# Warming products on any free PSUM bank until the seventh f-tile, and attention pairs of the third batch on in a fixed order

## The chip, the cores and the metric

One core of one Trainium2 chip runs the whole problem. The engines named here are TensorE (PE, whose weight loads the profile lists apart as PEld), VectorE (DVE), ScalarE (ACT), GpSimd (POOL) and SyncE (SP), which issues nearly all transfers. The metric is device microseconds of one execution, shown as a median of a few runs; one further execution was profiled, and all rows below come from that one.

## The reference

The program is an attention with fixed masks, followed by a gated two-layer network on its result. All inputs and the output are float32 (the two weight matrices arrive as float64 numbers, because they were divided by a NumPy square root).

```python
def _attn_ref(q, k, v):                       # q, k, v: (8 batches, 8 heads, 576, 64)
    scores = scale * np.matmul(q, k.transpose(0, 1, 3, 2))
    rel = pos[:, None] - pos[None, :]
    mask_local = (rel >= 0) & (rel < 32)                       # heads 0-3
    mask_strided = (rel >= 0) & (pos[None, :] % 32 == pos[:, None] % 32)   # heads 4-7
    scores = np.where(masks, scores, -1e9)
    attn = softmax(scores)
    return np.matmul(attn, v)

def _moe_ref(x, w_in, w_out):                 # x: (4608, 512), w_in: (512, 2048), w_out: (2048, 512)
    h = x @ w_in
    sp = np.maximum(h, 0.0) + np.log1p(np.exp(-np.abs(h)))
    return (h * erf(sp)) @ w_out
```

## The kernel before

**Attention** is done a pair of heads at a time: `heads(b, hp, ...)` for batch `b` (0 to 7) and head pair `hp` (0 and 1 local mask, 2 and 3 strided), 32 pairs in all, written here as 1.3 for batch 1, pair 3. Each pair has: two loads (queries and keys, values), `scores` on PE with the mask added by a product with the identity (the first 8 pairs) or by DVE (the rest), the row maximum (DVE, L408), the exponential (ACT, L429 or, piece by piece with its sum, L444), the reciprocal of the sum (L462, L463) and the scaling by it (POOL or DVE, L470), the transposes on PE (`turn`, L479), their copy to SBUF (ACT, L485), the product with the values (`av`, L498), and the split of the result into a high part (ACT, L517) and a low part (DVE, L522) that the network reads as `xhi` and `xlo`. There are four such pairs of tiles, one for each head pair, each with a ring of two batches.

**The network** works on 12 chunks of 384 tokens by 16 tiles of 128 hidden features: 192 f-tiles. `ftile` has 12 products of 384 columns (`mm1`, L641: high times high, high times low, low times high), eleven pointwise steps that alternate between ACT (L649, L679) and DVE (L646, L676, L682), the last of which writes `glo`, and nine products of 512 columns into the three output banks `o0`, `o1`, `o2` (`mm2`, L712). Three PSUM banks (`h`) hold the f-tiles under way, so the first product of f-tile 3 waits for `glo` of f-tile 0. The first three chunks are cut into segments of 4, 4 and 8 features, so that the first 12 f-tiles need only 4 + 4 of the 32 weight tiles. A weight tile is loaded as 64-bit words and becomes two float32 tiles: three bit operations on DVE (L591, L598, L604), a cast on ACT (L609) and a difference on DVE (L612). `wN` is tile N: 0 to 15 are `w_in`, 16 to 31 `w_out`.

**SBUF and PSUM at the start.** The first two batches are computed before any f-tile can run, and seven of their eight pairs borrow room: `home` names weight tiles whose SBUF place holds the pair's queries, keys, values and probabilities first, so the load of, for example, `w14` (home of pair 1.2) can only be issued once `av` of pair 1.2 is done. `banks` names the PSUM banks they use: those of `h`, `o0`, `o1`, `o2`, or the two banks `ps`.

**What sets the order.** Nothing is written out by hand. Every piece of work is an `Op` with an engine, a duration, a key, and the buffers and ops it depends on. `Plan.order` is a list scheduler: on each engine it looks at the first `WINDOW` ops by key, takes the one that can start soonest in its own model of time, and among those that can start within 2 ns the one with the lowest key. The result is the fixed order of instructions of each engine; on the chip each engine then works strictly down its list, and SP its list of transfers. The keys are tables of numbers: `KP` (one row a pair, with seven steps), `KW` (weight tiles), `FT` (steps of an f-tile), and `PRO + SLOT * k` for f-tile k.

**The filler.** When the planner finds PE idle it can put in a warming product: one bf16 product of the identity with 512 columns of constants (L824), whose result nobody reads. Before the change it writes one buffer in bank `o2`, and it ends with the first pair that uses that bank (pair 0.3):

```python
first = plan.add("pe", 0.217, -10.0, warm, o_con, [warm_ps])
plan.filler = (first, warm, warm_ps, o2_first[0])
```

There are 14 of them.

Of the kernel before, what the change touches and what calls it, by code (L numbers as in the profile page):

```python
# [38 lines left out]
)  # L39
KP = (  # L40
    (20.3287, 53.91, -160.53, 18.1965, -47.9251, -48.4351, -45.9709),
    (-11.5867, -179.324, 278.004, -56.864, 29.5817, 111.268, -24.2757),
    (-37.2881, -285.525, 218.382, -3.34506, -147.536, -61.349, -160.866),
    (-3.30041, -73.2783, 113.183, 4.45478, -53.4418, -218.264, -9.86919),
    (18.4971, -63.2216, 140.85, -145.013, -40.5878, -375.486, -97.5485),
    (26.9473, -194.862, 187.13, -211.888, 100.567, -144.206, -385.178),
    (29.3598, 112.224, 34.5004, -139.626, -186.803, -311.65, -205.587),
    (40.629, -47.3516, -107.951, -152.785, -94.4726, -260.703, -328.673),
    (145.421, -29.1371, 101.451, 215.325, 141.627, 232.353, 147.006),
    (156.959, 213.968, -86.1117, 167.748, 197.693, 69.8737, 215.036),  # L50
    (214.158, 122.935, 213.19, 328.996, 214.474, 18.278, 173.207),
    (192.057, 302.789, 389.825, 207.406, 286.075, 210.654, 231.419),
    (311.012, 303.593, 285.037, 162.499, 316.839, 302.425, 213.801),
    (300.253, 202.803, 308.604, 234.138, 294.599, 227.375, 455.083),
    (234.305, 484.755, 266.452, 59.4845, -388.072, 255.135, 34.835),
    (365.686, 279.095, 257.584, 136.31, 289.522, 279.315, 239.144),
    (311.964, 379.917, 360.165, 318.437, 277.972, 289.912, 313.896),
    (398.277, 419.169, 405.134, 540.378, 463.219, 414.175, 410.718),
    (374.266, 340.595, 412.97, 365.306, 312.772, 421.745, 367.034),
    (400.873, 504.293, 447.42, 525.942, 542.714, 477.305, 404.891),  # L60
    (429.56, 205.119, 452.221, 477.615, 588.077, 437.589, 433.417),
    (434.951, 395.537, 444.904, 412.829, 464.795, 438.451, 436.011),
    (454.859, 440.736, 485.38, 513.585, 478.737, 465.682, 432.45),
    (466.926, 593.721, 523.838, 503.643, 416.953, 481.072, 489.414),
    (570.321, 596.524, 584.59, 533.102, 568.713, 632.717, 665.278),
    (481.13, 245.48, 404.828, 533.548, 417.461, 534.902, 474.017),
    (532.709, 540.879, 495.504, 473.216, 767.743, 414.442, 503.973),
    (602.088, 614.688, 620.304, 610.44, 682.554, 676.756, 678.331),
    (605.431, 617.475, 664.962, 621.689, 662.639, 578.048, 547.039),
    (690.641, 695.65, 723.32, 466.891, 705.997, 650.07, 429.58),  # L70
    (645.282, 705.753, 703.317, 687.525, 662.029, 631.987, 690.823),
    (700.543, 703.075, 661.128, 671.32, 528.806, 628.088, 603.928),
)
# [850 lines left out]
```

## Time and profile before

| | us |
|---|---|
| median of 3 runs (lowest, highest) | 938.94 (937.38, 939.02) |
| the profiled execution's own time | 937.39 |
| its span, first to last instruction | 935.6 |
| PE busy | 908.6 |
| DVE busy | 683.3 |
| ACT busy | 660.2 |
| POOL busy | 61.2 |
| first product of f-tile 0, of f-tile 3 | 49.92, 69.73 |
| first `mm2` | 71.93 |

Times in the rows are microseconds from the start of the span. A row of the timeline gives start, duration, engine, line, operation, what it writes and reads, and how often it stands there in a run; durations of PE and DVE rows overlap the next row's start a little, so the step from start to start is what an instruction costs its engine. A row of windows gives, for a stretch, the busy time of each engine with its number of instructions, the granted clock of PE (1.00 is full, 0.50 half), the busy share of the 16 DMA engines, and GB/s moved. In the page's slices a digit is tenths of one fortieth of the span (23.4 us).

### The profile page before, as it was taken

To read this page: it belongs to the slowest core of one execution; us is meant where nothing else is said; L and a number is where in the kernel's file an instruction comes from. 1 tells how busy PE (TensorE), PEld (TensorE's weight loads), DVE (VectorE), ACT (ScalarE), POOL (GpSimd) and SP (SyncE) were. 2 spreads that over 40 slices of the span, in tenths; PEclk is the share of its full clock that TensorE was granted. 3 is DMA by queue.
4 is the path that set the end of the run, shared out by engine and by line. 5 is a ranking of instruction groups with operands and counts; after the bars stand their busy time and mean duration, and the time that the engine had idled before them with its cause. 6 is when DMAs were issued, how large, how long until landed. Compare 5 with 4: busy or idle time off the path is not lost.

```text
span 935.6 us, 20064 instructions
## 1 busy us (share of the span) xinstructions
PE 908.6 (97%) x8157; PEld 810.6 (87%) x8158; DVE 683.3 (73%) x1355; ACT 660.2 (71%) x1478; POOL 61.2 (7%) x58
## 2 busy tenths in 40 slices
PE   4789999999999999999999999999999999999998
PEld 3578899988888899998898888989898888999997
DVE  6779999997588667657677686676776776666664
ACT  5667888777667767667676766766766767766765
POOL 1200012111112000000010000000100000000000
PEclk9589999999999999999999999999999999999999
DMA  9967114312415011001204111000211110000000
GB/s 346 350 246 291 39 61 66 64 29 50 97 54 143 18 46 61 0 28 64 72 27 140 41 53 55 35 27 18 89 46 46 62 56 18 34 1 1 34 1 34
DMA packets 23421, 68.86 MB, mean 74 GB/s; under 512 B 2592, under 2 KB 3232, under 8 KB 23328
## 3 DMA queue, kind: packets, MB, share of 16 engines
q1 hardware_dynamic: 20736, 62.86, 18.9%
q0 software_dynamic: 2592, 4.72, 3.6%
q8 instruction: 64, 1.05, 0.5%
q14 instruction: 29, 0.24, 0.1%
HBM read 53.41 MB, written 14.16 MB: 72 GB/s over the span
## 4 chain that ended last, share of the span: by engine, by line
PE 90%; DVE 5%; DMA 2%; issue 1%; ACT 0%; POOL 0%; SPq 0%; POOLq 0%; DVEq 0%
PE h L641 41%; PE o L712 41%; PE s L372 3%; PE x L498 3%; PE t L479 2%; DVE a L646 1%; DMA v<-v_loc 1%; DMA qk<-qk_loc 1%; PE s L498 1%; DVE pair L612 1%; DVE w L598 0%; DMA qk<-qk_str 0%; PE s L479 0%; DVE w L604 0%; DVE b L646 0%
## 5 line engine op out<-in xcount | busy, mean ns | idle before, releaser
L712 PE MATMUL o<-pair,ghi 128*128 128x512 f32 x1152 | 360.3, 394 | 0.0
L641 PE MATMUL h<-xhi,pair 128*128 128x384 f32 x1536 | 303.4, 340 | 0.3 <-DVE glo L682 0.2
L641 PEld LDWEIGHTS h<-xhi,pair 128*128 128x128 f32 x1536 | 270.1, 189 | 12.1 <-DVE glo L682 2.4
L712 PEld LDWEIGHTS o<-pair,ghi 128*128 128x128 f32 x1152 | 211.1, 188 | 36.0 <-ACT ob L727 0.4
L649 ACT ACTIVATE b<-b 128x384 f32<-128x384 f32 x384 | 201.1, 525 | 44.8 <-DVE b L646 40.7
L712 PE MATMUL o<-pair,glo 128*128 128x512 f32 x576 | 224.6, 390 | 0.0
L641 PE MATMUL h<-xlo,pair 128*128 128x384 f32 x768 | 165.1, 337 | 0.0
L646 DVE SCALAR_TENSOR_TENSOR a<-a,h 128x384 f32<-128x384 f32 x192 | 105.8, 551 | 70.5 <-ACT b L649 70.2
L649 ACT ACTIVATE a<-a 128x384 f32<-128x384 f32 x192 | 101.1, 527 | 75.5 <-DVE a L646 74.9
L682 DVE TENSOR_TENSOR glo<-h,ghi 128x384 fp32r<-128x384 f32 x192 | 106.5, 555 | 54.0 <-ACT ghi L679 53.6
L649 ACT ACTIVATE a<-h 128x384 f32<-128x384 f32 x192 | 93.3, 486 | 72.4 <-PE h L641 71.4
L646 DVE SCALAR_TENSOR_TENSOR a<-h,a 128x384 f32<-128x384 f32 x192 | 106.6, 555 | 44.0 <-ACT a L649 43.6
L676 DVE TENSOR_TENSOR h<-b,h 128x384 f32<-128x384 f32 x192 | 107.2, 558 | 43.0 <-ACT b L649 42.7
L641 PEld LDWEIGHTS h<-xlo,pair 128*128 128x128 f32 x768 | 136.6, 189 | 0.0
L712 PEld LDWEIGHTS o<-pair,glo 128*128 128x128 f32 x576 | 108.1, 188 | 23.3
L679 ACT CAST ghi<-h 128x384 fp32r<-128x384 f32 x192 | 90.9, 473 | 34.8 <-PE o L712 27.6
L646 DVE SCALAR_TENSOR_TENSOR b<-b,a 128x384 f32<-128x384 f32 x192 | 106.7, 556 | 2.5
L649 ACT ACTIVATE b<-a 128x384 f32<-128x384 f32 x192 | 100.6, 524 | 2.9
L470 POOL TENSOR_TENSOR sm<-sm,r 128x768 f32<-128x768 f32 (+3 forms) x35 | 45.4, 1298 | 633.2 <-DVE r L463 512.3
L408 DVE TENSOR_REDUCE mx<-s 128x12 f32<-128x768 f32 (+3 forms) x37 | 28.9, 786 | 8.0 <-PE s L385 7.7
L727 ACT COPY ob<-o 128x512 f32<-128x512 f32 x54 | 31.2, 587 | 4.2 <-PE o L712 4.0
L372 PEld LDWEIGHTS s<-qk 64*32 64x32 f32 (+1 forms) x1616 | 21.2, 117 | 11.6 <-issue 5.0
(49 smaller groups left out, 513.9 us busy)
## 6 DMA issues: line engine op xcount, KB each, us to landing
out<-ob SPq DMA_DIRECT2D x36, 256.0 KB, 2.0
v<-v_loc SPq DMA_DIRECT2D x13, 640.0 KB, 3.8
words<-w_out SPq DMA_DIRECT2D x16, 512.0 KB, 8.8
words<-w_in SPq DMA_DIRECT2D x16, 512.0 KB, 7.9
qk<-qk_loc SPq DMA_DIRECT2D x13, 592.0 KB, 3.8
qk<-qk_str SPq DMA_DIRECT2D x12, 608.0 KB, 4.1
v<-v_str SPq DMA_DIRECT2D x16, 384.0 KB, 3.1
out<-ob POOLq DMA_DIRECT2D x18, 256.0 KB, 4.6
```

Source lines behind the costliest of these rows:

```text
L372: yield nc.tensor.matmul(bank(s, h)[m * j : m * (j + 1), 64 * t : 64 * (t + 1)], queries(rows, q0, m), keys_of(rows, q0), start=(h, j) not ...
L408: yield nc.vector.tensor_reduce(out=mx[:, parts[i], :units], in_=wide(of(s, i)), axis=mybir.AxisListType.X, op=ALU.max)
L470: yield (nc.gpsimd if pool_norm else nc.vector).tensor_tensor(out=d, in0=d, in1=spread(rc, i), op=ALU.mult)
L498: yield nc.tensor.matmul(bank(px, m)[h * D : (h + 1) * D, a * n : (a + 1) * n], values(rows, (2 * a + h) * D), pt[rows, h, c : c + n], sta ...
L641: yield nc.tensor.matmul(ph[:, :CH], win[4 * s + cc][:, w, fs], x[cc][:, c0 : c0 + CH], start=(i == 0), stop=(i == len(terms) - 1))
L646: yield nc.vector.scalar_tensor_tensor(out=out, in0=in0, scalar=scalar, in1=in1, op0=op0, op1=op1)
L649: yield nc.scalar.activation(dst, src, func, bias=bias[i], scale=scale)
L676: yield nc.vector.tensor_tensor(out=ph[:, :CH], in0=bb.tile, in1=ph[:, :CH], op=ALU.mult)
L679: yield nc.scalar.copy(ghi.tile, ph[:, :CH])
L682: yield nc.vector.tensor_tensor(out=glo.tile, in0=ph[:, :CH], in1=ghi.tile.bitcast(F32), op=ALU.subtract)
L712: yield nc.tensor.matmul(po.tile, g[:, ts], wout[f][:, w], start=(f == first_f and i == 0), stop=(f == last_f and i == 2),)
L727: yield nc.scalar.copy(ob.tile, po.tile)
```

## The change

Three things change in the code. A warming product is no longer tied to one buffer: `_spare` asks, for each of the tags `o2`, `o1`, `o0` and `ps`, whether the last buffer there has no user left at that time, and the filler makes a new buffer on the first such bank. The filler ends with `mm1` of the seventh f-tile (`mm1_first[6]`) and no longer with pair 0.3. And the pairs from batch 2 on (those that are not `own`) are chained: each pair's loads, scores, transposes and value products come after the same step of the pair before (`turns`). The planner's look-ahead `WINDOW` goes from 250 to 400, and all its tables (`PRO`, `SLOT`, `FT`, `KW`, `KP`) are replaced.

```diff
-PRO = 40
-SLOT = 4.3
+PRO = 41
+SLOT = 4.59
 BACKLOG = 1.1130116
-FT = (-10.5854, -2.40059, 6.35438, 31.1122, -70.6188, 13.8691, 84.3288, 11.3161, 2.23209, -15.3397, 0.274502, 44.5287)
+FT = (0.289363, -24.4893, -7.52371, 20.6488, -54.5891, -7.75633, 107.462, 111.082, -9.24549, -68.1746, -106.267, 36.4614)
...
-    (700.543, 703.075, 661.128, 671.32, 528.806, 628.088, 603.928),
+    (-30, -22.5012, -29.7906, -30, -30, -28.8058, -28.8058),
...
-    WINDOW = 250
+    WINDOW = 400
...
+    def _spare(self, tag, live, now):
+        order = live.get(tag)
+        return not order or all(
+            u.end is not None and u.end + (self.SAME if u.eng == "pe" else self.LATENCY)["pe"] <= now
+            for u in order[-1].users
+        )
...
                 if e == "pe" and self.filler and self.filler[0].end is not None:
-                    can.append((max(free[e], self.filler[0].end + 0.2), 1e9, e, -1))
+                    soon = max(free[e], self.filler[0].end + 0.2)
+                    spare = [tag for tag in self.filler[2] if self._spare(tag, live, soon)]
+                    if spare:
+                        can.append((soon, 1e9, e, -1))
...
-                o = Op(e, 0.217, 0.0, self.filler[1], (), (), (self.filler[2],), 0.0)
+                x, emit = self.filler[1](next(tag for tag in self.filler[2] if self._spare(tag, live, t)))
+                o = Op(e, 0.217, 0.0, emit, (), (x,), (), 0.0)
...
+        if not own:
+            for name, o in (("q", lq), ("v", lv), ("s", o_s), ("t", o_t), ("x", o_v)):
+                if name in turns:
+                    o.after.append(turns[name])
+                turns[name] = o
...
-    warm_ps = buf("ps_o", f"o{NTT - 1}", [P, DM], "warm")
-
-    def warm():
-        yield nc.tensor.matmul(warm_ps.tile, ident_b, con[:, :512], start=True, stop=True)
-
-
-    first = plan.add("pe", 0.217, -10.0, warm, o_con, [warm_ps])
-    plan.filler = (first, warm, warm_ps, o2_first[0])
+    def warm(tag):
+        n = len(plan.ops)
+        w = buf("ps_a", "ps", [P, 2, 512], f"warm{n}") if tag == "ps" else buf("ps_o", tag, [P, 512], f"warm{n}")
+
+        def run():
+            yield nc.tensor.matmul(w[:, 0, :] if tag == "ps" else w[:, :], ident_b, con[:, :512], start=True, stop=True)
+
+        return w, run
+
+    w, run = warm("o2")
+    first = plan.add("pe", 0.217, -10.0, run, o_con, [w])
+    plan.filler = (first, warm, ("o2", "o1", "o0", "ps"), mm1_first[6])
```

The lists of instructions show what the planner makes of it. Lines that are 11 to 17 higher in the changed kernel are the same statements (L498 is L509 there, L641 is L658, L712 is L729, L824 is L841). The first place is PE where the opening passes into the f-tiles. Names carry the batch and pair (`s_1_3` are the scores of pair 1.3, `h_0` is f-tile 0); only the first row of a run that repeats is shown. Before:

```order
L641 MATMUL h_0_787<-xhi0_76,pair0_363 128x384
L372 MATMUL s_1_3_816<-qk30_1_3_622,qk29_1_3_621 64x64 x24
L498 MATMUL s0_1_0_575<-qk11_1_0_286,v_1_0_368 64x32 x2
L641 MATMUL h_1_899<-xhi0_76,pair0_363 128x384
L641 MATMUL h_2_971<-xhi0_76,pair0_363 128x384
L498 MATMUL s_1_3_816<-qk29_1_3_621,v_1_3_687 64x54 x22
L641 MATMUL h_3_1103<-xhi0_76,pair0_363 128x384
```

And with the change:

```order
L383 MATMUL s_1_3_851<-qk30_1_3_738,qk29_1_3_737 64x64 x24
L509 MATMUL s0_1_0_629<-qk11_1_0_545,v_1_0_675 64x32 x2
L841 MATMUL warm3794_927<-con_85 128x512
L841 MATMUL warm3803_1007<-con_85 128x512
L658 MATMUL h_0_1073<-xhi0_76,pair0_943 128x384
L658 MATMUL h_1_1113<-xhi0_76,pair0_943 128x384
L509 MATMUL s_1_3_851<-qk29_1_3_737,v_1_3_883 64x54 x22
L658 MATMUL h_2_1203<-xhi0_76,pair0_943 128x384
L841 MATMUL warm3824_1278<-con_85 128x512
L658 MATMUL h_3_1313<-xhi0_76,pair0_943 128x384
L658 MATMUL h_4_1339<-xhi0_76,pair0_943 128x384
L729 MATMUL o0_0_1364<-pair16_549,ghi_0_1283 128x512 x2
```

The scores of pairs 1.3 and 1.2 and the value products of pair 1.0 have moved ahead of f-tile 0, and f-tile 4 and the scores of pair 2.0 ahead of the first `mm2`. The rows of warming products stand for 9 (ahead of the scores of pair 1.2), 21 and 10 of them; there are 82 in the changed kernel.

The second place is DVE around the `glo` of the first two f-tiles. Before:

```order
L646 SCALAR_TENSOR_TENSOR a_1_988<-a_1_988,h_1_899 128x384
L682 TENSOR_TENSOR glo_0_1043<-h_0_787,ghi_0_1032 128x384
L646 SCALAR_TENSOR_TENSOR a_2_1005<-h_2_971,a_2_1005 128x384
L646 SCALAR_TENSOR_TENSOR b_1_1018<-b_1_1018,a_1_988 128x384
L612 TENSOR_TENSOR pair19_995<-w32_19_966,pair19_995 128x512
L598 SCALAR_TENSOR_TENSOR w32_6_968<-words6_730,w32_6_968 128x512
L522 TENSOR_TENSOR xlo3_83<-s_1_3_816,xhi3_79 128x18x18
L522 TENSOR_TENSOR xlo3_83<-s_1_3_816,xhi3_79 128x18x14
L676 TENSOR_TENSOR h_1_899<-b_1_1018,h_1_899 128x384
```

And with the change:

```order
L621 SCALAR_TENSOR_TENSOR w32_7_1135<-words7_776,w32_7_1135 128x512
L699 TENSOR_TENSOR glo_0_1298<-h_0_1073,ghi_0_1283 128x384
L693 TENSOR_TENSOR h_1_1113<-b_1_1220,h_1_1113 128x384
L615 SCALAR_TENSOR_TENSOR w32_23_1139<-words23_843,w32_23_1139 128x512
L663 SCALAR_TENSOR_TENSOR a_2_1272<-a_2_1272,h_2_1203 128x384
L699 TENSOR_TENSOR glo_1_1332<-h_1_1113,ghi_1_1329 128x384
L663 SCALAR_TENSOR_TENSOR b_2_1311<-b_2_1311,a_2_1272 128x384
L608 TENSOR_SCALAR w32_14_1337<-words14_1222 128x512
L629 TENSOR_TENSOR pair7_1304<-w32_7_1135,pair7_1304 128x512
```

More stands ahead of `glo_0` than before (the splits of pairs 1.3 and 1.2, one weight tile, two steps of f-tiles 1 and 2), less between `glo_0` and `glo_1`, and the first bit operation on weight tile 14 now follows two rows after `glo_1`; before, it comes some 70 rows later.

The third place is the list of transfers that SP issues, around tile 14. Before:

```order
L585 DMA words12_1075<-w_in 128x1024
L358 DMA v_2_0_1118<-v_loc 128x1280
L585 DMA words14_1130<-w_in 128x1024
L585 DMA words15_1146<-w_in 128x1024
L585 DMA words27_1169<-w_out 128x1024
```

And with the change:

```order
L602 DMA words10_1171<-w_in 128x1024
L602 DMA words30_1199<-w_out 128x1024
L602 DMA words14_1222<-w_in 128x1024
L602 DMA words15_1274<-w_in 128x1024
L361 DMA qk_2_1_1290<-qk_loc 128x1184
```

The load of tile 14 keeps its place among the last weight tiles (it needs the room of pair 1.2), and has moved ahead of tile 12 in the list.

More of the change, by code (lines that the diff above doesn't have):

```diff
@@ L26 @@
 SW = 512
-PRO = 40
-SLOT = 4.3
+PRO = 41
+SLOT = 4.59
 BACKLOG = 1.1130116
-FT = (-10.5854, -2.40059, 6.35438, 31.1122, -70.6188, 13.8691, 84.3288, 11.3161, 2.23209, -15.3397, 0.274502, 44.5287)
+FT = (0.289363, -24.4893, -7.52371, 20.6488, -54.5891, -7.75633, 107.462, 111.082, -9.24549, -68.1746, -106.267, 36.4614)
 KI = 6.0
 KW = (
[4 rows of a table removed]
[4 rows of a table added]
 )
 KP = (
[L41 to L71, printed above, removed]
-    (700.543, 703.075, 661.128, 671.32, 528.806, 628.088, 603.928),
@@ new lines @@
+    (8.72531, 15.3266, 49.3756, 8.39434, 9.71023, 16.0435, 40.2649),
+    (-33.2667, -32.4582, -25.2032, -4.71525, 23.3634, 38.5999, -34.6194),
+    (-3.32722, 14.171, 65.6986, 22.708, 5.7846, -0.90524, -6.13492),
+    (-0.845554, 25.7345, 14.5624, 4.32498, 9.67501, 24.2441, 58.6052),
+    (27.1808, 31.0972, 28.9995, -1.24966, -22.602, 24.5694, -9.17578),
+    (12.7444, 8.33475, 64.1615, 7.47789, 24.3066, 31.2506, -7.37547),
+    (59.1669, 75.8282, 35.2304, 54.1156, 3.55879, 6.30503, 1.44202),
@@ new lines @@
+    (48.539, 42.13, 43.9807, 7.065, 28.0374, 12.7742, 20.1927),
+    (62.9708, 118.313, 65.7316, 109.482, 135.689, 178.053, 214.067),
+    (123.636, 279.712, 105.738, 148.596, 187.83, 145.11, 237.33),
+    (133.667, 215.051, 137.96, 168.378, 198.152, 176.116, 238.661),
+    (142.144, 208.148, 235.957, 308.305, 263.348, 272.387, 283.229),
+    (247.917, 257.392, 254.975, 251.721, 255.925, 267.187, 270.083),
+    (245.277, 289.199, 303.979, 299.482, 291.447, 309.453, 340.687),
+    (287.063, 331.064, 291.825, 315.285, 298.122, 317.411, -28.8058),
@@ new lines @@
+    (300.054, -18.1776, 308.518, 308.574, 313.179, 338.852, -5.16791),
+    (302.28, 24.0747, 350.314, 380.417, 330.366, 13.1796, 0.905989),
+    (368.813, 1.91996, 389.598, 30, 26.6243, 11.6485, 30),
+    (388.986, 23.6787, 26.4176, 30, 30, 30, 30),
+    (-30, 22.7877, 22.7877, -9.32161, 7.48325, 22.7877, -4.17841),
+    (30, -29.3034, -29.3034, -30, 28.8694, 30, -24.7335),
+    (1.13668, 26.6544, -26.6503, 14.6547, -28.061, -27.5337, -27.5337),
+    (-30, -30, -30, -15.006, -17.1047, -20.5063, -28.8058),
@@ new lines @@
+    (-9.559, -7.17764, 30, -8.11829, 28.8694, -10.2326, -27.8205),
+    (24.655, 25.2704, 25.2704, 25.4731, 24.8511, 25.2704, 25.3122),
+    (11.5661, -21.8954, 10.424, 14.8671, -26.0021, -18.3975, -12.9881),
+    (27.7249, 12.8171, 27.7249, 27.7249, 12.7777, 22.8153, 23.4476),
+    (15.8312, 24.7146, 25.4392, 26.4798, -25.8351, 30, -30),
+    (-7.01186, -6.66902, 4.91674, 7.32403, -7.79962, -6.61799, -6.95783),
+    (-29.2688, 28.0581, -29.7906, -30, -30, -28.796, -28.8058),
+    (-20.7485, -13.2027, -21.6073, -26.2752, -30, -28.8058, -28.8058),
@@ L559, in heads @@
             first.append(o)
+            o_t = o
             o = add("act", act(384 * (p.stop - p.start), 0.06), k_t + (0.1 + e), fetch(i), [o], [], [y, slab])
@@ L763, in attention_moe @@
     o_ps, order_o, stored = [None] * NTT, [None] * NTT, {}
-    x_of, w_load = {}, []
+    x_of, w_load, turns = {}, [], {}
     mm1_of, mm1_first, hi_of = {}, [], []
@@ L794, in chunks_of @@
         return [0, 1] if b % 2 == 0 else [1, 2]
-    last_av, o2_first = [], []
+    last_av = []
     for b in range(B):
@@ L806, in attention_moe @@
                 last_av.append(o)
-                if banks and "o2" in banks and not o2_first:
-                    o2_first.append(o_s)
                 for n, f in enumerate(home or ()):
```

8 rows, old and new, of the table KW are left out of this document.

## The prediction

> **What bounds the kernel now.** I read the page first, then windows of 6 us over the opening, then the timelines of PE and DVE there, and the end of the chain of waits. The page and the chain:
>
> ```profile
> span 935.6 us, 20064 instructions
> PE   4789999999999999999999999999999999999998
> PEclk9589999999999999999999999999999999999999
> PE 90%; DVE 5%; DMA 2%; issue 1%; ACT 0%; POOL 0%; SPq 0%; POOLq 0%; DVEq 0%
> 921.82 10.21 PE o L712 x45
> ```
>
> PE is full from the fourth slice on and sets the end: its last product ends at 921.82 + 10.21 = 932.03, and 937.39 - 932.03 = 5.36 us of the profiled time lie outside that. From then on the amount of PE work decides, and no order changes it. What an order can change is the opening, the first three slices, where the clock is low too. The windows:
>
> ```profile
> 0.00:6.00 6.00, 0.00 (x0) 0.00 (x0) 1.46 (x3) 1.49 (x2) 0.30 (x5) 1.00 0.68 229
> 6.00:12.00 6.00, 5.45 (x138) 3.52 (x140) 3.62 (x7) 1.25 (x2) 0.00 (x0) 1.00 1.00 361
> 12.00:18.00 6.00, 4.33 (x68) 2.57 (x65) 5.23 (x18) 3.90 (x23) 2.50 (x3) 1.00 1.04 402
> 18.00:24.00 6.00, 1.38 (x47) 1.09 (x47) 5.96 (x13) 6.00 (x30) 1.78 (x2) 0.71 1.03 395
> 24.00:30.00 6.00, 5.10 (x223) 4.25 (x224) 5.18 (x12) 2.97 (x14) 1.11 (x1) 0.72 0.99 358
> 30.00:36.00 6.00, 4.62 (x127) 3.61 (x126) 2.89 (x9) 3.01 (x18) 0.87 (x2) 0.56 0.97 334
> 36.00:42.00 6.00, 2.72 (x36) 1.84 (x26) 4.17 (x13) 5.15 (x24) 2.07 (x2) 0.50 0.95 332
> 42.00:48.00 6.00, 4.59 (x115) 4.12 (x117) 5.30 (x13) 2.45 (x5) 1.95 (x2) 0.50 1.00 378
> 48.00:54.00 6.00, 6.00 (x63) 5.84 (x59) 2.62 (x5) 1.18 (x3) 0.00 (x0) 0.50 0.45 180
> 54.00:60.00 6.00, 6.00 (x166) 5.00 (x168) 5.08 (x11) 5.71 (x23) 0.00 (x0) 0.94 0.25 65
> 0.00:68.50 68.50, 45.30 (x1021) 35.96 (x1026) 49.92 (x119) 40.44 (x160) 12.06 (x16) 0.78 0.86 312
> ```
>
> The columns after the length are busy PE, weight loads, DVE, ACT, POOL, then clock, DMA share, GB/s. Three things: the clock is at 0.50 from 36 to 54; DMA is full until 48; DVE is busy only 49.92 of the first 68.5 us, so 18.6 us of it are lost. Who loses it, from the timelines of DVE and then of PE:
>
> ```profile
> 32.35 0.82 DVE L408 TENSOR_REDUCE mx<-s 128x10 f32<-128x640 f32 x1 [3.10 <-PE s L385]
> 37.77 0.89 DVE L408 TENSOR_REDUCE mx<-s 128x5 f32<-128x320 f32 x2 [2.05 <-PE s L385]
> 50.21 0.82 DVE L522 TENSOR_TENSOR xlo<-s,xhi 128x256 fp32r<-128x256 f32 x2 [2.88 <-ACT xhi L517]
> 54.67 0.56 DVE L646 SCALAR_TENSOR_TENSOR a<-h,a 128x384 f32<-128x384 f32 x1 [1.83 <-ACT a L649]
> 67.98 0.55 DVE L682 TENSOR_TENSOR glo<-h,ghi 128x384 fp32r<-128x384 f32 x1
> 73.96 0.55 DVE L646 SCALAR_TENSOR_TENSOR b<-b,a 128x384 f32<-128x384 f32 x1
> 74.43 0.69 DVE L604 SCALAR_TENSOR_TENSOR w<-words,w 128x512 uint32<-128x512 uint32 x1
> 75.03 0.76 DVE L591 TENSOR_SCALAR w<-words 128x512 uint32<-128x512 uint32 x2
> ```
>
> ```profile
> 41.83 1.54 PE L479 MATMUL s<-ident,sm 128*128 128x128 f32 x6 [2.56 <-POOL sm L470]
> 49.92 2.91 PE L641 MATMUL h<-xhi,pair 128*128 128x384 f32 x8
> 52.63 1.48 PE L641 MATMUL h<-xlo,pair 128*128 128x384 f32 x4
> 65.75 0.88 PE L479 MATMUL s<-ident,sm 128*128 128x128 f32 x6 [2.75 <-POOL sm L470]
> 69.73 1.67 PE L641 MATMUL h<-xhi,pair 128*128 128x384 f32 x8
> 71.93 0.62 PE L712 MATMUL o<-pair,ghi 128*128 128x512 f32 x2
> ```
>
> Of the DVE idle time after 28 us, four waits make 9.9 us (3.10, 2.05, 2.88, 1.83), all for PE or for ACT waiting on PE. PE is slow there: f-tile 0 takes 4.2 us at half clock (49.92 to 54.11), f-tile 3 takes 2.2 (69.73 to 71.93); six transposes 1.54 against 0.88. The row at 67.98 is `glo` of f-tile 0, done at 68.53; the first `mm2` is at 71.93, and PE does not stop again: 932.03 - 71.93 = 860.1 us.
>
> **The change part by part.**
>
> *Warming products.* The lists show 82 for 14, so 68 more. One costs PE:
>
> ```profile
> 10.99 2.75 PE L824 MATMUL warm<-con 128*128 128x512 bf16 x12
> ```
>
> 2.75 / 12 = 0.23 us at most, 15.6 us for 68. They all stand ahead of f-tile 3 and nearly all ahead of f-tile 0, where PE was busy 45.3 of 68.5 us, so 23.2 us of idle time cover them. Without that cover each would cost its 0.23. The two groups ahead of f-tile 0 (9 and 21) take 6.9 us in which PE would otherwise wait for the weights of that f-tile. What they buy is the clock.
>
> [...]
>
> *The first `glo`.* DVE has more ahead of it now: one more weight tile (four instructions; 0.60 is the step from 74.43 to 75.03, 0.34 for the first one, half of the pair of 0.76 less overlap: 2.1 us), two f-tile steps (0.47 from 73.96 to 74.43: 0.9) and four splits of pairs 1.3 and 1.2 (0.82 for two: 1.6), less one small one of 0.2: +4.4 us. So `glo` of f-tile 0 ends at 49.92 + 4.4 + lost time. If DVE loses as much as before (18.6): 72.9. If only the first wait for a weight tile is lost (DVE's first 4.5 us, 1.46 busy in the first window): 58.8. Those are the outer bounds.
>
> A nearer bound comes from the transfers. The scores of pair 1.3 now stand ahead of f-tile 0, and the load of their queries and keys is the last of 13.1 MB in SP's list (added up with the sizes on the page). When that lands, and what follows, from these rows:
>
> ```profile
> 24.01 1.40 PE L372 MATMUL s<-qk 64*32 64x64 f32 x80 [3.88 <-DMA qk<-qk_loc]
> 57.81 0.31 ACT L444 ACTIVATE sm<-s,mx 128x64 f32<-128x64 f32 x1
> 61.01 0.36 ACT L444 ACTIVATE sm<-s,mx 128x64 f32<-128x64 f32 x1
> 54.15 0.49 ACT L649 ACTIVATE a<-h 128x384 f32<-128x384 f32 x1 [3.36 <-PE h L641]
> ```
>
> The transfer that landed at 24.0 had 7.3 MB up to itself, and the windows add up to 8.3 MB by then, so a load lands when about 1 MB more has moved. 14.1 MB have moved at 41 us (12.5 by 36, 14.5 by 42). Then, one after the other: scores and mask 1.9, value products of pair 1.0 1.4, their two splits 0.8, a weight cast 0.5, the piecewise exponential of pair 1.3 3.5 (57.81 to 61.3), two casts 1.0, DVE's difference 0.6, f-tile 0 2.2, its first tanh 0.4: 53.3, against 54.15 + 0.4 before. That looks like little, but the 3.5 us of pair 1.3 and most of pair 1.2 lie behind the tanh before and ahead of it now. From the tanh to the end of `glo`, DVE's list has some 9.4 us (nine f-tile steps 4.2, six weight operations 3.1, four splits 1.6, one scaling 0.5), against 68.53 - 54.67 = 13.9 before. So 62.7 with no further wait. I take 64.3, 1.6 us for hand-overs between engines; that is a lost time of 10 us on DVE, which is 18.6 less 8.6 of the 9.9 named above.
>
> *To the end.* Behind `glo` 0 come `prod`, a weight operation, an f-tile step and `glo` 1 (3 x 0.47 + 0.60 = 2.0), then f-tile 4 (2.2 and a hand-over of 0.15), because f-tile 4 needs that bank and now stands ahead of the first `mm2`: 68.65. PE's work from there is 860.1 less f-tile 4 (2.2) and the scores of pair 2.0:
>
> ```profile
> 89.07 1.04 PE L372 MATMUL s<-qk 64*32 64x64 f32 x80
> ```
>
> So 860.1 - 3.2 = 856.9, PE ends at 925.55, and with 5.36 the profiled time is 930.9, 6.5 us less. The first `mm2` may be late by 3.2 us against 71.93 before anything is lost: break-even is `glo` 0 at 70.8. Counted in the list by the steps above, DVE has 67.2 us of work from `glo` 0 to `glo` 16 and PE 65.0 between the matching `mm2`; the 4.35 us between `glo` 0 and the first `mm2` cover the 2.2, so PE does not starve.
>
> *The fixed order of later pairs.* It moves work within the full PE, 24 pairs with the same products. The nearest scores-to-transposes distance stays two f-tiles in both lists (3.1: f-tile 54 to 56; before 5.0: 91 to 93), and the tightest hand-over, value products of pair 2.3, has three `mm2` steps (2.0 us) ahead of f-tile 48, which reads the result. Splits take 0.8 on ACT and 0.4 more on DVE. I cost it at 0, hidden behind those `mm2`; without cover it would be about 1.2 us at each of two places. A gain is excluded, since PE has no idle time there.
>
> The three runs lie at 937.38, 938.94 and 939.02, the profiled one at the low end; I add 1.1 of the 1.55 between it and the median: 932.0.
>
> **The rivals.**
>
> *The clock falls all the same* (chance 0.14). The planner sees full speed and constant transfer rates; on the chip the groups pass early and PE still stands idle. For it: the low clock at 4.59 us of work in 6. Against: 30 products in two groups are 6.9 us in a row. Price at half clock ahead of `glo` 0: f-tile 0 2.0, transposes 0.66, and 0.3 each for scores and value products: about 3 us, so 933.9 profiled, 935.0 in the median.
>
> *The lost time moves instead of shrinking* (0.14). DVE's waits are then for transfers: DMA is full to 48 in both, and loads come in another order. DVE loses some 16.5, `glo` 0 is at 70.8, no change: 938.5. Against: none of the four waits names DMA.
>
> *Tile 14 blocks DVE* (0.12, slower). DVE's second row behind `glo` 1 now waits for weight tile 14, whose load SP may issue only after the value products of pair 1.2. DVE works in order, so f-tiles 2 and 3 stand behind it and PE runs dry.
>
> ```profile
> SPq L585 <- PE s L498: 27.6, 4, 14.6
> words<-w_in SPq DMA_DIRECT2D x12, 512.0 KB, 7.9
> ```
>
> SP has lost 27.6 us to such waits, and a tile lands 7.9 us after its issue. Those products ended at 69.73 before; so late again, tile 14 lands at 77.6. DVE is there 2.5 us behind `glo` 0, and break-even is 73.3: each us past that is lost in full, 4.3 here: 941.7 profiled, 942.8 in the median. By the forecast they end near 57, and the 22.6 MB up to tile 14 have moved near 64 (17.7 by 54 before, at 0.37 a us from 48 on), while DVE comes at 66.8. So it needs 9 us of delay, but the margin for the forecast itself is 3 us.
>
> **How the numbers follow.** The forecast has 0.60: 929.2 profiled at the bound of 62.7, 930.9 at 64.3, 934 at 67.5; in medians 929.5 to 935. The clock rival adds 935, the second 938.5, the third 942.8. The range 928 to 939.6 leaves out the slower rival and a little below. What a measurement can tell from no change is 0.2%, 1.9 us: faster (below 937.06) is the forecast and the clock rival, 0.74; the same 0.14; slower 0.12.
>
> **What would show it.** Right: PEclk at 1.00 in nearly all of the first 68 us; the four DVE waits shorter; `glo` 0 near 64, the first `mm2` near 69, and about 857 us of PE without a stop behind it. Wrong: a half-clock stretch between 36 and 54; a DVE wait for `words` near 65; PE idle time behind the first `mm2`, near f-tiles 48 or 64 above all, which would mean that the fixed order is not free; or a first `mm2` at 69 with an end that has not moved.

## The result, and the profile after

The change makes the kernel slower. The median of four runs is 948.70 us (948.03 to 950.17) against 938.81 us of the kernel before on the same chip; the ratio is 1.0111, with a 95% interval of 1.0093 to 1.0128. I had forecast 932.0 with a range of 928 to 939.6, so the result lies outside the range and on the other side. The profiled execution took 948.81 us, 11.42 more than before.

The page of the kernel after: its span, PE and its clock in 40 slices, and the shares of the chain of waits.

```profile
span 947.0 us, 20224 instructions
PE   6899999999999999999999999999999999999998
PEclk9999999999999999999999999999999999999999
PE 86%; DVE 6%; DMA 3%; issue 2%; ACT 2%; SPq 1%; POOL 0%; DVEq 0%; POOLq 0%
```

The change does what it says: the granted clock is 1.000 in the mean of the span, where it was 0.983 before. The price is in PE's timeline of the opening (L841 is the warming product, L658 `mm1`, L729 `mm2`):

```profile
10.25 6.42 PE L841 MATMUL warm<-con 128*128 128x512 bf16 x15
49.69 3.84 PE L841 MATMUL warm<-con 128*128 128x512 bf16 x9
55.91 8.58 PE L841 MATMUL warm<-con 128*128 128x512 bf16 x20 [0.27 <-PE s L396]
64.14 1.75 PE L658 MATMUL h<-xhi,pair 128*128 128x384 f32 x8
74.80 4.28 PE L841 MATMUL warm<-con 128*128 128x512 bf16 x10
78.73 1.74 PE L658 MATMUL h<-xhi,pair 128*128 128x384 f32 x8
83.08 0.62 PE L729 MATMUL o<-pair,ghi 128*128 128x512 f32 x2
```

Twenty products (the list has 21 there; the trace holds records of 80 of all 82) take 8.58 us, nine take 3.84: 0.43 each, where twelve took 2.75 before, 0.23 each. The chain of waits shows how one follows the other:

```profile
56.35 0.39 PE warm L841
56.74 0.04 issue
56.78 0.39 PE warm L841
```

Each runs for 0.39 us and the next one begins 0.04 behind its end. Before, one lasted 0.38 us (median) and the next began 0.23 behind its start: they overlapped. The list of instructions with its waits shows why: before, all 14 products write one buffer and wait for nothing; now each has a buffer of its own, and nearly all of them wait for PE's own semaphore (`PE_49` below). Inside a group each begins those 0.04 us behind the end of the product before, which wrote the old buffer of the same bank.

```order
L841 LDWEIGHTS con_85
L841 MATMUL warm3758_219<-con_85 128x512 [waits PE_49]
L841 LDWEIGHTS con_85
L841 MATMUL warm3759_222<-con_85 128x512 [waits PE_49]
```

So f-tile 0 starts at 64.14 (before 49.92), f-tile 3 at 78.73 (69.73), the first `mm2` at 83.08 (71.93). That is 11.15 us, and the profiled time grew by 11.42. VectorE, which waits for the scores of pair 1.2 behind the nine products and for f-tile 0 behind the 20, in its timeline and in a window that ends with `glo` of f-tile 0:

```profile
55.52 0.56 DVE L419 TENSOR_REDUCE mx<-s 128x6 f32<-128x384 f32 x1 [1.25 <-PE s L396]
57.81 2.46 DVE L629 TENSOR_TENSOR pair<-w,pair 128x512 fp32r<-128x512 f32 x2
67.15 0.56 DVE L663 SCALAR_TENSOR_TENSOR a<-h,a 128x384 f32<-128x384 f32 x1 [3.68 <-ACT a L666]
76.15 0.56 DVE L699 TENSOR_TENSOR glo<-h,ghi 128x384 fp32r<-128x384 f32 x1
```

```profile
0.00:76.71 76.71, 62.44 (x1231) 37.39 (x1234) 54.61 (x129) 43.77 (x168) 11.21 (x16) 1.00 0.83 303
```

DVE has 54.61 us of work up to there (I had worked out 54.3) and loses 22.1; I had said it would lose 10, and it lost 18.6 before. Behind 84 us PE waits four more times, 1.5 us in all and 0.6 at most, as the view of waits has it:

```profile
PE h L658 <- DVE glo L699: 1.5, 4, 0.6
```

### The profile page after: what moved, and what is told of

It is laid out like the page before. It is cut to its first block, busy times and chain, and to the rows that moved or that the text cites. A ratio compares the mean times of both kernels' runs of the same rounds, so it can differ in the third digit from the quotient of the medians.

```text
span 947.0 us, 20224 instructions
## 1 busy us (share of the span) xinstructions
PE 927.4 (98%) x8224; PEld 810.0 (86%) x8226; DVE 687.2 (73%) x1355; ACT 659.3 (70%) x1478; POOL 60.3 (6%) x58
## 3 DMA queue, kind: packets, MB, share of 16 engines
q8 instruction: 64, 1.05, 0.5%
## 4 chain that ended last, share of the span: by engine, by line
PE 86%; DVE 6%; DMA 3%; issue 2%; ACT 2%; SPq 1%; POOL 0%; DVEq 0%; POOLq 0%
PE h L658 39%; PE o L729 37%; PE x L509 3%; PE s L383 3%; PE warm L841 2%; PE t L490 1%; DMA qk<-qk_str 1%; DVE a L663 1%; DVE b L663 1%; PE s L509 1%; ACT b L666 1%; DMA qk<-qk_loc 1%; DVE glo L699 1%; DMA out<-ob 1%; DVE h L693 1%
## 5 line engine op out<-in xcount | busy, mean ns | idle before, releaser
L729 PE MATMUL o<-pair,ghi 128*128 128x512 f32 x1152 | 360.5, 394 | 0.0
L658 PE MATMUL h<-xhi,pair 128*128 128x384 f32 x1536 | 303.0, 339 | 1.5 <-DVE glo L699 1.5
L658 PEld LDWEIGHTS h<-xhi,pair 128*128 128x128 f32 x1536 | 268.7, 188 | 16.2 <-DVE glo L699 6.3
L729 PEld LDWEIGHTS o<-pair,ghi 128*128 128x128 f32 x1152 | 211.0, 188 | 36.5 <-ACT ob L744 1.3
L729 PE MATMUL o<-pair,glo 128*128 128x512 f32 x576 | 224.6, 390 | 0.0
L658 PE MATMUL h<-xlo,pair 128*128 128x384 f32 x768 | 164.4, 336 | 0.0
L666 ACT ACTIVATE a<-h 128x384 f32<-128x384 f32 x192 | 93.2, 485 | 76.7 <-PE h L658 76.1
L658 PEld LDWEIGHTS h<-xlo,pair 128*128 128x128 f32 x768 | 136.0, 188 | 0.0
L729 PEld LDWEIGHTS o<-pair,glo 128*128 128x128 f32 x576 | 108.1, 188 | 23.4
L663 DVE SCALAR_TENSOR_TENSOR b<-b,a 128x384 f32<-128x384 f32 x192 | 108.8, 567 | 1.2
L841 PE MATMUL warm<-con 128*128 128x512 bf16 x80 | 30.1, 377 | 4.2 <-PE s L396 0.3
```

The source lines that it names most:

```text
L658: yield nc.tensor.matmul(ph[:, :CH], win[4 * s + cc][:, w, fs], x[cc][:, c0 : c0 + CH], start=(i == 0), stop=(i == len(terms) - 1))
L663: yield nc.vector.scalar_tensor_tensor(out=out, in0=in0, scalar=scalar, in1=in1, op0=op0, op1=op1)
L666: yield nc.scalar.activation(dst, src, func, bias=bias[i], scale=scale)
L729: yield nc.tensor.matmul(po.tile, g[:, ts], wout[f][:, w], start=(f == first_f and i == 0), stop=(f == last_f and i == 2),)
L841: yield nc.tensor.matmul(w[:, 0, :] if tag == "ps" else w[:, :], ident_b, con[:, :512], start=True, stop=True)
```

## The experiments

Theory A is the price: each product waits for the one before, and the groups stand in front of work that is ready. Theory B is the new order of the opening: it is worse by itself. All times are medians; a ratio is against the kernel before in the same job. Openings of two profiles differ by up to 1.6 us with nothing changed ahead of that place (the last experiment), so smaller differences between the times of single instructions are not read.

**One buffer for a run of products.** The plan keeps its order, instruction for instruction, on all five engines; only the waits go.

```diff
-                x, emit = self.filler[1](next(tag for tag in self.filler[2] if self._spare(tag, live, t)))
-                o = Op(e, 0.217, 0.0, emit, (), (x,), (), 0.0)
+                tag = next(tag for tag in self.filler[2] if self._spare(tag, live, t))
+                last = live[tag][-1] if live.get(tag) else None
+                x, emit = self.filler[1](tag, last)
+                o = Op(e, 0.217, 0.0, emit, (), () if x is last else (x,), (x,) if x is last else (), 0.0)
...
```

> The changed kernel with one edit: a warming product that follows another one on the same bank writes the buffer of that one again, and takes a new buffer only where something else had the bank between. The order of the instructions is the same on all five engines, all 82 warming products included; only the waits of PE on its own semaphore ahead of them go. Theory A (each warming product waits for the one before because its buffer is new, so it costs 0.43 us from start to start where 0.22 was priced, and the groups ahead of f-tile 0 and f-tile 3 sit in front of work whose operands are there): the nine-product groups take 2.0 us and not 3.8, the 20 ahead of f-tile 0 take 4.4 and not 8.6, the 10 ahead of f-tile 3 take 2.2 and not 4.3; the first mm2 comes 7 to 12 us earlier than 83.1, at 71 to 76, and the time is 934 to 942 us. Theory B (the new order of the opening itself is 10 us worse, and the warming products only fill waits that are there anyway): the groups get shorter, PE waits longer behind them, first mm2 stays at 81 to 83.5 and the time at 946 to 949.

Measured 942.42 us, a little above what theory A gave; ratio 1.0027 (1.0014 to 1.0039). In its job the kernel before took 939.75, so 2.7 us are left of 9.9: 7.2 go. PE's and DVE's timelines and DVE's window up to `glo` 0:

```profile
53.85 4.48 PE L849 MATMUL warm<-con 128*128 128x512 bf16 x20
57.98 1.76 PE L660 MATMUL h<-xhi,pair 128*128 128x384 f32 x8
68.80 2.33 PE L849 MATMUL warm<-con 128*128 128x512 bf16 x9
75.14 0.62 PE L731 MATMUL o<-pair,ghi 128*128 128x512 f32 x2
...
70.23 0.55 DVE L701 TENSOR_TENSOR glo<-h,ghi 128x384 fp32r<-128x384 f32 x1
```

```profile
0.00:70.78 70.78, 54.38 (x1230) 38.81 (x1238) 55.42 (x129) 43.70 (x168) 11.23 (x16) 0.98 0.88 329
```

Twenty take 4.48 us and not 8.58, and the first `mm2` comes 7.94 us earlier. The wait on the old buffer is shown as the cause of that part, since nothing else differs. The first `mm2` is still 3.2 us later than before. That alone need not cost anything, because f-tile 4 and the scores of pair 2.0, 3.2 us of work, now lie ahead of it; but the time is above that before by more than the noise, so theory A is not all of it.

**The kernel before, with a buffer for each of its 14 products.** Its order is unchanged.

```diff
-                o = Op(e, 0.217, 0.0, self.filler[1], (), (), (self.filler[2],), 0.0)
+                x, emit = self.filler[1]()
+                o = Op(e, 0.217, 0.0, emit, (), (x,), (), 0.0)
...
```

> The kernel before with one edit: each of its 14 warming products writes a new buffer of bank o2, as in the change; the order of the instructions is the same. Theory A: the 12 products that took 2.75 us (0.23 each) take 12 x 0.43 = 5.1 us, 2.4 us more, and they stand ahead of work that waited for transfers there: the time is between 0 and +2.5 us against the kernel before. If the buffer has nothing to do with the step, the 12 still take 2.75 us.

```profile
11.16 5.91 PE L826 MATMUL warm<-con 128*128 128x512 bf16 x13
```

13 products take 5.91 us, 0.45 each: the same step in another kernel. The time is 939.58, ratio 0.9991 (0.9981 to 1.0001): some 3 us more of PE cost nothing that can be measured there, though in the one profiled execution the first `mm2` is 1.9 us later. In the changed kernel the same price was 7.2 us of the time.

**The changed kernel with the first 14 products alone, and with the planner told the true price.**

```diff
+    left = 14
     for op in plan.order():
+        if op.emit.__name__ == "run":
+            left -= 1
+            if left < 0:
+                continue
```

```diff
-                o = Op(e, 0.217, 0.0, emit, (), (x,), (), 0.0)
+                o = Op(e, 0.43, 0.0, emit, (), (x,), (), 0.0)
...
```

> The changed kernel without its last 68 warming products: only the first 14, as many as before the change, are issued; everything else stands in the changed order. Theory A: 68 times 0.43 = 29 us of PE go, of which some 10 to 20 were on the path; against it the clock falls back to half somewhere between 28 and 54 us, so that the first products of the f-tiles cost double for 3 us; first mm2 at 70 to 77, time 935 to 942. Theory B: the time stays at 946 to 950, since the order is the cause. A third one, C (the clock is what decides the opening): without the warming products the f-tiles start later than 64 us, and the time is 950 or more.

> The changed kernel with the planner told 0.43 us for a warming product instead of 0.217, so that it puts in 42 and not 82, each still with a buffer of its own. Theory A: the planner's own mistake goes, the groups end when the work behind them is ready, and the time falls to 936 to 943 with first mm2 at 72 to 78. Theory B: 946 to 949, as in the change.

Measured 944.66, ratio 1.0045 (1.0027 to 1.0062), and 944.07, ratio 1.0043 (1.0025 to 1.0061); both lie between theories A and B. With 68 products fewer, the first `mm2` comes at 78.16, still 6.2 us later than before, and f-tile 0 waits in PE for its own weights:

```profile
56.45 1.65 PE L658 MATMUL h<-xhi,pair 128*128 128x384 f32 x4 [1.91 <-ACT pair L626]
58.81 1.01 PE L658 MATMUL h<-xhi,pair 128*128 128x384 f32 x2 [0.71 <-DVE pair L629]
```

So the price of the products is not all. This run can't tell how much of the rest is the new order (theory B) and how much the clock, which is 0.81 up to 70.78 us here and 0.98 in the one-buffer kernel: the last four products of f-tile 0 take 1.48 us against 0.86 there, and f-tiles 3 and 4 take 5.8 (from 72.31) against 4.3. With the true price (42 products) the first `mm2` is at 74.49, but this plan puts f-tile 4 behind it again, and PE waits 4.5 us from there on (3.4 for `glo`, 1.1 for an output bank).

**Which groups stand in front of ready work.** The one-buffer kernel, without the 11 products ahead of the scores of pairs 1.3 and 1.2, and without the 31 ahead of f-tiles 0 and 3 (the products are skipped by their number where the plan is emitted).

```diff
+        if op.eng == "pe":
+            pe += 1
+            if op.emit.__name__ == "run":
+                n += 1
+                if 41 <= n <= 51:
+                    continue
...
```

In the other kernel the condition is `n > 51`.

> The one-buffer kernel (the changed order, 82 warming products that write one buffer in a run; 942.4 us, first mm2 at 75.1) without the 11 warming products that stand ahead of the scores of pairs 1.3 (2) and 1.2 (9). They take 2.3 us there, and VectorE's row maximum of pair 1.2 waits 1.79 us for those scores, with the last weight tile of f-tile 0 queued behind it. Theory A2 (the warming products still stand in front of ready work at that place): scores of 1.2 come 2 us earlier, the weight tile is ready near 56.5 and not 58.4, glo of f-tile 0 near 69, the time is 940 to 941. Theory B2 (the new order itself makes f-tile 0 late: its last weight tile is converted behind the maxima of pair 1.2, whose queries land late): scores stay at 50 to 53 and the time at 942 to 943.5.

> The one-buffer kernel without the 31 warming products that stand ahead of f-tile 0 (21) and f-tile 3 (10), where they take 4.5 and 2.3 us. Theory A2: f-tile 0 starts up to 4 us earlier, first mm2 at 70 to 72, time 938 to 940. Theory B2 (the weight tile, converted at 58.4, and the bank of f-tile 0, free with its glo at 70.8, are what f-tiles 0 and 3 wait for, and the warming products fill those waits): first mm2 stays within 1 us of 75.1 as long as the clock stays up; time 941.5 to 944.

The first: 940.64, ratio 1.0005 (0.9991 to 1.0019), first `mm2` at 74.31. The time is the one that theory A2 gave, and it can no longer be told from the kernel before: beside products that are cheap and out of the way, the new order costs nothing that can be measured here. The second: 943.79, ratio 1.0047 (1.0030 to 1.0064), first `mm2` at 77.98, so theory A2 is wrong there; theory B2 had the time right, and the first `mm2` nearly 2 us too early. Its PE:

```profile
58.27 1.01 PE L660 MATMUL h<-xhi,pair 128*128 128x384 f32 x2 [1.98 <-DVE pair L631]
...
72.12 1.68 PE L660 MATMUL h<-xhi,pair 128*128 128x384 f32 x8 [1.95 <-DVE glo L701]
```

Without the products PE waits, for the weight tile and for the bank. The clock falls too: it is 0.86 from 60 to 72 us against 1.00 in the one-buffer kernel, the last four products of f-tile 3 take 1.45 us (from 73.63) against 0.86, and the way from `glo` 0 to the first `mm2`, with f-tiles 3 and 4 on it, takes 5.9 us against 4.4. At the price of 0.22 those two groups fill idle time, as I had said, and the clock that they hold is worth some 1.5 us there (an estimate, 5.9 less 4.4); at 0.43 they did not, and the ten ahead of f-tile 3 ran 2.4 us past `glo` 0 (76.71 to 79.08).

**The filler without the new tables, and 14 products more in the old order.**

```diff
-    WINDOW = 400
+    WINDOW = 250
-        if not own:
+        if False:
...
-    (8.72531, 15.3266, 49.3756, 8.39434, 9.71023, 16.0435, 40.2649),
+    (20.3287, 53.91, -160.53, 18.1965, -47.9251, -48.4351, -45.9709),
...
```

These lines are against the one-buffer kernel: the new filler stays, and it gets all tables of the kernel before and no fixed order. The other is the kernel before with 14 products put into its finished order, ahead of PE's 22nd piece of work, the scores at 24 us:

```diff
+EXTRA = {21: 14}
...
-    for op in plan.order():
+    ops = plan.order()
+    for op in plan.fill(ops, ("o2", "o1", "o0", "ps"), more, mm1_first[6]):
```

> The kernel before with its own tables and look-ahead and without the fixed order of later pairs, with the new filler on any free bank until the seventh f-tile, one buffer for a run of warming products: 66 of them, in places that the planner chooses (it moves some of the early work on the other engines too). The question is what the filler does without the new tables. If a held clock is worth the 6 us that I had put on the opening: 932 to 936. If the opening is set by transfers and by the order on VectorE: 937 to 942.

> The kernel before, instruction for instruction, with 14 more warming products (one buffer) in the one place where TensorE waits 3.9 us for a transfer, ahead of the scores at 24 us. They take 3.1 us, so they cost nothing, and TensorE is busy from 18.75 to 31 but for a fraction. If the activity right before is what sets the clock, it is 1.00 until about 31 and not 0.5 from 20.5 to 27.4; the pieces there (scores 1.40, value products 1.44) get 1.3 us shorter in all. Theory A2/B2 alike: the opening is set later, so the time is 937.5 to 940.5. If an early clock carries through to the end: 935 to 937.

The old tables with the new filler: 951.21, ratio 1.0129 (1.0104 to 1.0155). The planner then puts 39 products between f-tiles 2 and 3, and behind the first `mm2` PE waits 7.0 us; which part weighs more I did not separate. The old order with 14 more: 938.99, ratio 0.9997 (0.9984 to 1.0009), no change. My expectation on the clock was wrong in place: it was 0.60 while the products ran, and 1.00 from 27.4 to 36, behind them.

**What the order does to f-tile 0.** In the changed kernel weight tiles 4 and 6, which f-tile 12 is the first to read, are loaded and converted ahead of 2 and 3, which f-tile 0 reads. Three kernels exchange their places.

```diff
+    for i, j in ((2, 4), (3, 6)):
+        for a, b in zip(w_ops[i], w_ops[j]):
+            place[id(a)], place[id(b)] = b, a
...
```

> The one-buffer kernel (942.4 us, glo of f-tile 0 at 70.8) with the places of four weight tiles exchanged: tile 2 takes the place of tile 4 in the loads, the bit operations, the cast and the difference, and 3 that of 6. Tiles 2 and 3 are read by f-tile 0, tiles 4 and 6 from f-tile 12 on, so what f-tile 0 needs is converted by 51 us and not 58.4; nothing else moves. Theory W (the new order is bad because it converts tiles 4 and 6 ahead of 2 and 3): VectorE's wait for the cast near 57 goes, glo of f-tile 0 comes 1 us earlier (it cannot be more here, the 21 warming products stay ahead of f-tile 0), time 940.5 to 941.5. Theory D (VectorE's own list, full from 53.7 us on, sets glo): no change, 942 to 943.

> The same exchange of tiles, without the 11 warming products ahead of the scores of pairs 1.3 and 1.2 (without the exchange that kernel took 940.6 us, glo of f-tile 0 at 69.95). Theory W: another 1 us less, 939 to 940. Theory D: no change, 940 to 941.5.

> The exchange of tiles, without the 32 warming products ahead of the scores of pairs 1.3 and 1.2 and ahead of f-tile 0; the 10 ahead of f-tile 3 stay. f-tile 0 can start at 52 to 54 us, 4 to 5 us earlier than in the one-buffer kernel. Theory W: its first tanh step is on VectorE near 57 and not at 61.5, glo near 66, first mm2 near 71, time 936.5 to 938.5. Theory D: VectorE has the maxima, sums and scalings of pair 1.2 and two weight tiles ahead of that step and reaches it no earlier than 60, so glo stays at 69 to 70 and the time at 940 to 942.

Measured 942.68 (ratio 1.0032, 1.0019 to 1.0045), 940.37 (1.0014, 1.0002 to 1.0025) and 941.78 (1.0027, 1.0018 to 1.0037). The first two gain nothing over the kernels without the exchange (942.42 and 940.64); the third has no such partner, and theory W had given it 936.5 to 938.5. Theory W falls. The third shows why, in PE's and DVE's timelines:

```profile
52.55 2.60 PE L663 MATMUL h<-xhi,pair 128*128 128x384 f32 x8
54.98 0.87 PE L663 MATMUL h<-xlo,pair 128*128 128x384 f32 x4
```

```profile
53.10 0.55 DVE L421 TENSOR_REDUCE mx<-s 128x6 f32<-128x384 f32 x1
...
55.39 2.46 DVE L631 TENSOR_TENSOR pair<-w,pair 128x512 fp32r<-128x512 f32 x2
...
59.59 0.54 DVE L466 TENSOR_REDUCE r<-sm 128x6 f32<-128x384 f32 x1
...
60.96 0.52 DVE L668 SCALAR_TENSOR_TENSOR a<-h,a 128x384 f32<-128x384 f32 x1
...
71.86 0.55 DVE L704 TENSOR_TENSOR glo<-h,ghi 128x384 fp32r<-128x384 f32 x1
```

f-tile 0 is finished at 55.85, 4.6 us earlier than in the one-buffer kernel, but DVE reaches its first step at 60.96 (61.53 there). From the maximum of pair 1.2 on it has 7.9 us of work in its list ahead of that step: maxima, differences, sums and scalings of pair 1.2 and two weight tiles. (Some 1.2 us of that is one weight difference that takes 1.86 us and not 0.68; in the changed kernel, which has the same pair of rows, it starts at 57.81, just behind a scaling on POOL that runs for 1.47 us from 57.66; that the two hinder each other was not tried.) Its `glo` 0 comes at 72.41, later than theory D's 69 to 70 too: without the products ahead of f-tile 0 the clock is 0.80 from 60 to 72 us (1.00 in the one-buffer kernel), f-tile 1 takes 3.8 us against 2.3 there, and DVE waits for ACT three times behind its first step (0.60, 0.92 and 0.36 us).

**No products between 26 and 51 us.** The one-buffer kernel without numbers 17 to 51, so that the clock falls.

```diff
+            if 17 <= n <= 51:
+                continue
...
```

> The one-buffer kernel without its 35 warming products 17 to 51 (those between 26 and 51 us), keeping the first 16 and the 31 ahead of f-tiles 0 and 3. The clock falls to half from some 20 us until the group ahead of f-tile 0. If a full clock in the attention part is worth what I put on it (3 us and more): 945 to 946. If the products there stand in front of as much work as they speed up: 940 to 943.

941.38, ratio 1.0014 (1.0003 to 1.0024), no slower than with them. The windows from 20 to 48 us, of the one-buffer kernel and then of this one, and this one's DVE up to `glo` 0:

```profile
20.00:48.00 28.00, 21.25 (x622) 15.22 (x613) 21.48 (x56) 18.55 (x81) 6.57 (x7) 0.94 0.92 352
```

```profile
20.00:48.00 28.00, 20.54 (x552) 16.32 (x550) 20.36 (x54) 18.83 (x82) 6.57 (x7) 0.63 0.87 324
...
0.00:70.05 70.05, 52.61 (x1199) 39.56 (x1203) 55.31 (x129) 43.74 (x168) 11.22 (x16) 0.85 0.90 336
```

The clock is 0.63 and not 0.94 there, and `glo` 0 is done at 70.05 against 70.78, a difference too small to read. In this order the products of the attention part, with the clock that they hold, are worth nothing that can be measured: if they speed anything up, they take it back by standing in the way. What the clock would be worth without them, no run shows.

**Taking work out of DVE's list.** The kernel just shown, with five operations of weight tiles 7 and 23 moved to behind `glo` 1: four that stood ahead of `glo` 0, and one just behind it. This run was to tell apart whether DVE's list or what it waits for sets `glo` 0.

```diff
+    for i in (7, 23):
+        for k, o in enumerate(w_ops[i][1:]):
+            o.start = max(o.start, glos[1].start + 0.001 * (k + 1) + 0.0001 * i)
...
```

> The kernel without warming products 17 to 51 (941.4 us, glo of f-tile 0 at 70.05, first mm2 at 74.4) with five operations of VectorE moved: the bit operations of weight tile 7 (three) and the first two of tile 23, which are read from f-tile 12 on, come behind glo of f-tile 1 and not ahead of glo of f-tile 0. By the steps in the trace that takes 0.34 + 0.34 + 0.60 + 0.60 = 1.9 us out of VectorE's list ahead of that glo. Theory D (VectorE's own list sets glo): glo near 68.2, first mm2 near 72.5, time 939.0 to 940. Theory D2 (VectorE stays full until some 200 us, so what it gives here it owes later): glo near 68.2, but TensorE's waits for glo behind the first mm2 grow from 1.7 us to 3 or more, time 940.5 to 942. Theory T (transfers or TensorE set glo): no change in glo, 941 to 942.

942.02, ratio 1.0037 (1.0023 to 1.0050). Its DVE, PE and PE's waits behind the first `mm2`:

```profile
59.15 0.52 DVE L668 SCALAR_TENSOR_TENSOR a<-h,a 128x384 f32<-128x384 f32 x1
67.04 0.56 DVE L704 TENSOR_TENSOR glo<-h,ghi 128x384 fp32r<-128x384 f32 x1
...
72.78 0.62 PE L735 MATMUL o<-pair,ghi 128*128 128x512 f32 x2
...
PE h L663 <- DVE glo L704: 3.0, 6, 1.1
```

`glo` 0 comes 2.45 us earlier, but 1.6 of that lies ahead of the moved operations (the first step at 59.15 against 60.79), so the edit itself gave 0.8 of its 1.9. The first `mm2` is 1.6 earlier and the end is not: PE's waits for `glo` grow from 1.7 to 3.0, the longest new one 1.1 us at 78.12. That is theory D2. DVE's column, the third after the length, says why in these windows of the one-buffer kernel:

```profile
60.00:72.00 12.00, 11.95 (x222) 10.00 (x222) 11.96 (x28) 10.60 (x24) 0.00 (x0) 1.00 0.58 188
...
84.00:200.00 116.00, 114.68 (x741) 101.84 (x740) 114.39 (x229) 93.55 (x200) 12.61 (x13) 1.00 0.27 58
```

It is nearly full up to 200 us, so work moved to behind `glo` 0 is owed a few f-tiles later. I take it that only what DVE loses ahead of 54 us could be gained, but no run here gains it: no kernel beat the one before.

## Why the prediction was wrong

Where the numbers went, each from the rows above (DVE's loss is the window's length less its busy time):

| | predicted | after | one buffer | before |
|---|---|---|---|---|
| DVE's work up to `glo` 0 | 54.3 | 54.6 | 55.4 | 49.9 |
| DVE's loss up to it | 10.0 | 22.1 | 15.4 | 18.6 |
| `glo` 0 done | 64.3 | 76.7 | 70.8 | 68.5 |
| from there to the first `mm2` | 4.4 | 6.4 | 4.4 | 3.4 |
| first `mm2` | 68.7 | 83.1 | 75.1 | 71.9 |
| from there to PE's end | 856.9 | 860.4 | 860.9 | 860.1 |
| profiled time | 930.9 | 948.8 | 941.4 | 937.4 |

1. *"2.75 / 12 = 0.23 us at most"* is the step that failed first. The row was right, but it is the price of a product that shares its buffer with the one before, and the change gives each its own: 0.43. The diff showed the new buffer, and the list with its waits showed the wait; I read the order without the waits. It cost 7.9 us at the first `mm2` and 7.2 of the 9.9 us of the time. The two groups ahead of f-tile 0, "6.9 us in which PE would otherwise wait", took 12.4.
2. *"So `glo` 0 at 64.3"* failed by another 6.5 us even at the price I assumed (70.8 in the one-buffer kernel). DVE's work (54.3) was right, and so was the list from the first tanh step to `glo` (9.4 worked out, 61.53 to 70.78 measured). The chain ahead of that step was not: I followed pair 1.3 to the weight cast and let the tanh step come at 53.3, but DVE's list has pair 1.2's maxima, sums and scalings ahead of it, 7.9 us from 53 to 61, even where f-tile 0 was finished at 55.85. A chain through transfers and PE said when the operand was there; the engine that reads it was full.
3. *"What they buy is the clock"*: they bought it (PEclk is 1.00 up to `glo` 0 at 76.71 us, and three of the groups have only two to four products; the rival that the clock falls is out), but I let it remove 8.6 of DVE's 18.6 us of loss. At the price of 0.23 the loss fell by 3.2, and a run with the clock at 0.63 between 20 and 48 us lost 14.7, no more than that one. The four waits "for PE" were put down to a slow PE. Ahead of three of them PE itself had stopped, for 2.09, 0.72 and 1.41 us (the last section); only the fourth is a slow PE alone, f-tile 0 at a clock of 0.50 from 49.92 to 54.11 us.
4. *"To the end"*: the 4.4 us between `glo` 0 and the first `mm2` are met in the one-buffer kernel; in the changed one the ten products ahead of f-tile 3 add 2.0. Behind it, "PE does not starve" was wrong by 1.5 us, in four waits at 133.6, 169.9, 266.8 and 421.9. The other 2.0 us (I took 3.2 off for work that now lies ahead; 1.2 came off) are steps that got a little longer: by the starts of PE's records, the same products of `mm2` take 1.3 us more in all, and those of `mm1` come down by 1.3 where f-tile 4's twelve should give 2.1. Why is open.
5. *The fixed order at 0*: two of those four waits lie where DVE is full anyway and two, 0.46 us together, behind 250 us. No run undoes the fixed order alone, so its part in the 1.5 us stays open.
6. *The slower rival*, tile 14 blocking DVE, did not happen: its first operation is at 79.07 with no wait. The side was wrong for a reason that none of the rivals held: each took 0.23 for granted. The break-even was out too. I had put it at `glo` 0 of 70.8; the one-buffer kernel has just that, and its profiled time is 4.0 us over that before, all of it in the term of 856.9, which came to 860.9 there.

## What to carry to other kernels

Price an instruction as the changed kernel will issue it, with its waits: the same product cost 0.22 or 0.43 us, and only the buffer it wrote differed. Ask of filler work whether it ends before the work behind it is ready: at 0.43 the ten products ahead of f-tile 3 ran 2.4 us past `glo` 0, and PE, which kept to its list, reached f-tile 3 only behind them. When you shorten a wait on a chain, look at the list of the engine that reads the result: DVE's was full, and of the 4.6 us by which f-tile 0 was finished earlier, 0.6 arrived at its first step there.
